# The four w_k transfers on ACT's queue, beside SP's w_mod transfers

## The chip, the cores and the metric

The kernel runs on one core of a Trainium2 chip. The metric is the device time of one launch in microseconds (us), as the median of several runs. A profile is one execution recorded by the hardware profiler; its times are counted from the start of its span.

## The reference

One block on x (2048 tokens, 512 features), all in float32: a linear attention (32 heads of 16) and a gated MLP that mixes over the tokens, each behind a layer norm whose scale, shift and gate come from a condition vector c.

```
mod = (silu(c) @ w_mod) -> sa, ca, ga, sb, cb, gb        # six vectors of 512
h = layernorm(x) * (1 + ca) + sa
q, k, v = h @ wqkv;  phi(t) = where(t > 0, t + 1, exp(t)) + 1e-6
o = phi(q) (phi(k)^T v) / (phi(q) sum phi(k) + 1e-6)     # per head
x = x + ga * (o @ wo)
h = layernorm(x) * (1 + cb) + sb
z1, z2 = halves of gelu(h @ w_in);  g = w_sp @ layernorm(z2) + b_sp
x = x + gb * ((z1 * g) @ w_out)
```

## The kernel before

Tokens are worked in 16 tiles of 128. Every float32 matmul operand is split into a high and a low part, and three matmuls (high by high, high by low, low by high; lines 110, 111 and 112) make one product. Before the first token tile can be multiplied, the kernel folds the condition into the projections: it needs `silu(c)` (`si`, lines 176 to 181), the vector ca as a column (`cm`, line 194, one call for each of the four 128-row parts of `w_mod[1]`), the same as a broadcast tile `cbr` on ACT (`mc`, line 326), the column means of the weights (`mr`, line 332, four calls for w_k, then four for w_q), and then on DVE the scaled weights (`wf`, line 336), which ACT and DVE split into the high and the low part (`qh`, line 340, and `qd` or `qg`, line 343). The first token matmuls are `kk1,0` and so on (lines 110 to 112, tile `kp`).

The order of all work is written out by hand in strings of short words (`ORDER`, `ORDER3`), and each engine runs its instructions in that order. `lm m,kc` loads part kc of `w_mod[m]`, `lk kc` loads part kc of w_k (the second of the three planes of `w_qkv`), `lw 0,h` a half of w_q, `ly t` a transposed tile of x (`xt`), `lx t` a plain one (`x`). `th t` and `tl t` split `xt` (ACT, line 399; DVE, line 402). `du` words are dummy matmuls on a tile of ones (line 172). All transfers are issued by SP: `dma = nc.sync.dma_start` at line 106, and the four of w_k through `load_part` at line 154, which `load_m` uses too. In the first line of `ORDER` the w_k loads stand behind the four loads of `w_mod[1]` and the words that use them:

```
si lm1,0 du1 du2 du3 du4 cm1,0 lm1,1 cm1,1 lm1,2 cm1,2 lm1,3 cm1,3 mc lk0 lk1 ly1 th1 tl1 lk2 lk3 du5
mr1,0 ly0 th0 tl0 lm0,0 mr1,1 mr1,2 lw0,0 lw0,1 ce1 mr1,3 wf1,3 qh1,3 qg1,3 mr0,0 ...
```

Buffers are chosen by hand as well: `SLOTS` holds for each pool one character for each tile that is asked for, in order, and that character names the buffer. A tile waits until the tile that held its buffer before has been read for the last time. The pool "zs" has 16 buffers and 83 requests.

Of the kernel before, what the change touches and what calls it, by code (L numbers as in the profile page):

```python
# [26 lines left out]
def block_kernel(ctx: ExitStack, tc: tile.TileContext, x, x_t, w_qkv, w_o, w_in, w_sp, b_sp, w_out,  # L27
                 w_out_tail, c, w_mod, ident_c, mask_c, out):
    nc = tc.nc

    def pool(name, bufs, space=None, stack=None):
# [27 lines left out]
            "25401567342067341564730642734206"  # L59
        ),  # L60
        "psb": "10101010010101001110101010101101010101",
        "zs": "0fe12dcba34987652dcb24a38b9a6cd8b4a3b838c4b6ca34cb34b4c3b4c30fe17b259d68a043cd6c0f1",
        "tb": (
            "065431260412304516230614250416450454653165013431423165104163421435241536211654063052141630516453"
            "0662635436360140660606656611141260606231515015"
# [18 lines left out]
    def sb(tag, shape, dt, name):  # L84
        return pools[tag].tile(shape, dt, tag=slot(tag), name=name)
# [20 lines left out]
    dma = nc.sync.dma_start  # L106
# [29 lines left out]
    RAW = {}  # L136
# [10 lines left out]
        XR[t] = sb("ta", [P, KC, P], F32, f"xt{t}")  # L147
        dma(XR[t], x_t[t])

    def load_part(key, src, kc, tag):  # L150
        k = key + (kc // 2,)
        if k not in RAW:
            RAW[k] = sb(tag, [P, 2, D], F32, "raw_" + "_".join(map(str, k)))
        dma(RAW[k][:, kc % 2], src[:, kc])

    def load_w(j, h):
        load_raw(("qkv", j, h), w_qkv[j, :, 2 * h:2 * h + 2, :])

    def load_wk(kc):
        load_part(("qkv", 1), w_qkv[1], kc, "st")  # L160

    def load_m(m, kc):
        load_part(("mod", m), w_mod[m], kc, "zs")
# [365 lines left out]
    def win_lo(h, kc, eng=nc.gpsimd):  # L529
# [4 lines left out]
    OPS = {  # L534
        "lx": load_x, "lw": load_w, "lm": load_m, "li": load_ident, "du": lambda k: dummy(2), "si": silu,
        "ly": load_xt, "lk": load_wk, "s1": s1, "bh": s2_hi, "bl": s2_lo, "cm": col_mm, "cr": col_part, "ce": col_end,
        "mc": mean_col, "mr": mean_mm, "wf": w_mid,
        "cv": lambda: (col_part("v"), col_end("v")), "mv": lambda m, k: mod_vec(m, k, k + 1), "vp": v_prod, "va": v_add,
# [232 lines left out]
    def hx_lo(t):  # L771
# [13 lines left out]
        "l5": lambda: load_mod(5, "s4"),  # L785
    })
    ORDER = """
        si lm1,0 du1 du2 du3 du4 cm1,0 lm1,1 cm1,1 lm1,2 cm1,2 lm1,3 cm1,3 mc lk0 lk1 ly1 th1 tl1 lk2 lk3 du5
        mr1,0 ly0 th0 tl0 lm0,0 mr1,1 mr1,2 lw0,0 lw0,1 ce1 mr1,3 wf1,3 qh1,3 qg1,3 mr0,0 yp0,0 lm0,2 wf1,1
        wf1,2 qh1,1 wf1,0 mr0,1 qh1,0 qd1,0 qg1,1 mr0,2 mr0,3 lm0,1 yp0,1 ya0,1 wf0,0 ly3 th3 qh1,2 qd1,2 lx0  # L790
        kk1,0 kk1,1 yp0,2 lm0,3 yp0,3 ya0,2 ya0,3 s10 ly2 kk0,0 kk0,1 wf0,1 wf0,2 th2 tl2 kk0,2 qh0,1 lx1
# [374 lines left out]
```

## Time and profile before

| | |
|---|---|
| median of 3 runs | 623.53 us (622.91 to 624.8) |
| profiled execution, its own time | 625.56 us |
| its span | 623.5 us |
| TensorE (PE) busy | 615.2 us, 99% of the span |
| VectorE (DVE) busy | 483.8 us, 78% |
| ScalarE (ACT) busy | 328.9 us, 53% |
| granted TensorE clock | 1.00 |
| read from HBM, written | 66.07 MB, 25.95 MB |

In the views, PE is the matmul stream and PEld its weight loads; SPq is the queue of SP, where a row is the time of issuing a transfer, not of the transfer. "to landing" counts from the issue to the arrival of the last byte. A bracket behind a row tells how long the engine sat idle before it and what ended that. The names of the rows are `raw_mod` for the parts of `w_mod`, `raw_qkv` for the parts of `w_qkv`, `pcol` for the column, `wm` for the means, `wf` for the scaled weights, `wk` and `wq` for their split parts.

### The profile page before, as it was taken

The page shows a single profiled execution, that of the slowest core. Times are in us where ns is not written, and L with a number is a line of the kernel's source. Part 1 is how long each engine was busy: PE and PEld are TensorE (multiplying, and loading weights), DVE is VectorE, ACT ScalarE, POOL GpSimd, SP SyncE. Part 2 cuts the span into 40 slices and gives each one's busy share as a digit, 9 for nine tenths or more (in the row PEclk, how much of TensorE's full clock was granted, in tenths as well). Part 3 has the DMA queues.
Part 4 walks back from the last instruction along what each step waited for, and adds up shares of the span by engine and source line. Part 5 has one row for each costly group of instructions (what it writes and reads, how often), then busy time and mean ns, then how long its engine had stood idle before and what let it go on. Part 6 is the DMA issues. An engine that isn't in the chain of part 4 may idle for free.

```text
span 623.5 us, 9515 instructions
## 1 busy us (share of the span) xinstructions
PE 615.2 (99%) x3383; PEld 559.2 (90%) x3383; DVE 483.8 (78%) x910; ACT 328.9 (53%) x556; POOL 221.8 (36%) x185
## 2 busy tenths in 40 slices
PE   8999999999999999999999999999999999999998
PEld 6678888787899999999999999999999999988886
DVE  2989997888888877877845689898799887886762
ACT  2768794656566476545647253654444354453320
POOL 0742354635866657553434504021223012400000
PEclk9999999999999999999999999999999999999999
DMA  8352422450337566746852966545575664889871
GB/s 275 147 185 79 156 91 74 125 158 33 102 92 177 138 168 178 202 145 191 234 181 80 307 235 209 152 139 107 171 204 169 188 159 145 239 282 272 265 260 67
DMA packets 91310, 105.74 MB, mean 170 GB/s; under 512 B 57120, under 2 KB 57632, under 8 KB 91264
## 3 DMA queue, kind: packets, MB, share of 16 engines
q1 hardware_dynamic: 91264, 105.15, 56.6%
q8 instruction: 26, 0.43, 0.3%
q14 instruction: 20, 0.16, 0.1%
HBM read 66.07 MB, written 25.95 MB: 148 GB/s over the span
## 4 chain that ended last, share of the span: by engine, by line
PE 80%; DMA 8%; DVE 7%; issue 2%; ACT 1%; SPq 0%; ACTq 0%; DVEq 0%
PE z L650 19%; PE P L928 17%; PE Pq L928 10%; PE pout L111 3%; PE pout L112 3%; PE pout L110 3%; PE po L110 2%; PE po L111 2%; PE po L112 2%; DMA raw_qkv<-in_w_qkv 2%; PE g L112 2%; PE qp L111 2%; PE qp L112 2%; PE g L110 2%; PE g L111 2%; PE qp L110 2%
## 5 line engine op out<-in xcount | busy, mean ns | idle before, releaser
L650 PE MATMUL z<-win,ht 128*128 128x344 f32 x768 | 122.7, 320 | 0.0
L650 PEld LDWEIGHTS z<-win,ht 128*128 128x128 f32 x768 | 121.5, 189 | 0.7
L928 PE MATMUL P<-z,f 128*128 128x344 f32 x576 | 96.3, 321 | 0.3
L928 PEld LDWEIGHTS P<-z,f 128*128 128x128 f32 x576 | 91.5, 188 | 1.5 <-DVE f L918 1.2
L918 POOL TENSOR_TENSOR f<-raw_wsp,f 128x512 fp32r<-128x512 f32 x24 | 35.9, 1509 | 148.4 <-ACT f L915 128.5
L928 PE MATMUL Pq<-z,wsp 128*128 128x344 f32 x384 | 61.3, 321 | 0.0
L928 PEld LDWEIGHTS Pq<-z,wsp 128*128 128x128 f32 x384 | 61.0, 188 | 0.0
L254 POOL TENSOR_TENSOR mv<-ve,mhalf 128x1 f32<-128x1 f32 x48 | 36.4, 760 | 41.8 <-DVE ve L253 30.5
L915 ACT ACTIVATE f<-raw_wsp 128x512 fp32r<-128x512 f32 x48 | 29.3, 626 | 32.3 <-DMA raw_wsp<-in_w_sp 12.9
L470 POOL TENSOR_TENSOR pksum<-pksum,tk 128x512 f32<-128x512 f32 x15 | 22.8, 1517 | 49.4 <-DVE tk L442 45.3
L915 ACT ACTIVATE f<-sa 128x512 fp32r<-128x512 f32 x36 | 22.5, 629 | 33.3 <-DVE sa L908 7.8
L268 ACT COPY uca<-us 128x768 uint16<-128x768 uint16 x32 | 25.1, 829 | 19.0 <-DVE us L983 12.2
L686 POOL TENSOR_TENSOR z<-zz,z 128x688 fp32r<-128x688 f32 x16 | 28.4, 1789 | 16.8 <-ACT z L683 16.8
L111 PE MATMUL pout<-wout,ut 128*128 128x512 f32 (+1 forms) x85 | 32.5, 382 | 0.6 <-DVE wout L1048 0.6
L110 PE MATMUL pout<-wout,ut 128*128 128x512 f32 (+1 forms) x85 | 32.4, 381 | 0.0
L112 PE MATMUL pout<-wout,ut 128*128 128x512 f32 (+1 forms) x85 | 32.3, 380 | 0.0
L1017 ACT ACTIVATE ut<-ur 128x384 fp32r<-128x384 f32 x32 | 15.2, 517 | 31.1 <-DMA ur<-ud 14.2
L918 DVE TENSOR_TENSOR f<-sa,f 128x512 fp32r<-128x512 f32 x36 | 26.0, 726 | 6.2 <-ACT f L915 6.0
L111 PE MATMUL qp<-wq,ht 128*128 128x512 f32 x64 | 25.3, 395 | 0.6 <-DVE wq L343 0.6
L110 PE MATMUL kp<-wk,ht 128*128 128x512 f32 x64 | 25.9, 404 | 0.0
L579 POOL TENSOR_TENSOR prod<-pq,zrep 128x512 f32<-128x512 f32 x16 | 21.4, 1342 | 11.7 <-ACT zrep L705 4.2
L112 PE MATMUL g<-pkhl,hhl 128*128 128x512 f32 x64 | 25.3, 395 | 0.2 <-DVE hhl L394 0.2
(254 smaller groups left out, 1500.1 us busy)
## 6 DMA issues: line engine op xcount, KB each, us to landing
raw_wsp<-in_w_sp SPq DMA_DIRECT2D x32, 512.0 KB, 4.5
ud<-uca SPq DMA_DIRECT2D x16, 384.0 KB, 3.1
ur<-ud SPq DMA_DIRECT2D x16, 384.0 KB, 4.5
z1d<-z SPq DMA_DIRECT2D x16, 344.0 KB, 2.5
zd<-zz SPq DMA_DIRECT2D x16, 344.0 KB, 3.0
z1r<-z1d SPq DMA_DIRECT2D x16, 344.0 KB, 3.7
xt<-in_x_t SPq DMA_DIRECT2D x16, 256.0 KB, 3.7
x<-in_x SPq DMA_DIRECT2D x16, 256.0 KB, 2.8
```

What stands on the lines that cost most here:

```text
L110: mm(o, a_hi, b_hi, start=first, stop=False, **kw)
L111: mm(o, a_hi, b_lo, start=False, stop=False, **kw)
L112: mm(o, a_lo, b_hi, start=False, stop=last, **kw)
L254: nc.gpsimd.tensor_tensor(mv[:, 1:2], ve, mhalf, op=OP.pow)
L268: nc.scalar.copy(pl[:, h], v[:, :, h])
L470: nc.gpsimd.tensor_add(pksum, pksum, PK[t])
L579: nc.gpsimd.tensor_mul(pr, PQ[t], KV["z"])
L650: mm(p[:, b, :HB], a[:, i, kc], win[h][:, j, kc, b * HB:(b + 1) * HB], start=kc == 0 and k == 0, stop=kc == KC - 1 and k == 2)
L686: nc.gpsimd.tensor_sub(Z2[t][:, 1], ZZ[t], f(Z2[t][:, 0]))
L915: nc.scalar.activation(SF[p, h, k][:, 0], s_src(p, h, k), AF.Copy)
L918: eng.tensor_sub(SF[p, h, k][:, 1], s_src(p, h, k), f(SF[p, h, k][:, 0]))
L928: mm(B[key][:, :HB], a[:, x_], b[:, y_], start=i == 1, stop=i == n)
```

## The change

The four `lk` words move to the very front of `ORDER`, ahead of `si`, and their transfers are issued from ACT's queue (`nc.scalar.dma_start`). Nothing else of the order changes. The string of the pool "zs" is written anew.

```
-        "zs": "0fe12dcba34987652dcb24a38b9a6cd8b4a3b838c4b6ca34cb34b4c3b4c30fe17b259d68a043cd6c0f1",
+        "zs": "0fed1234cba9876512341acb849c63284acb48b83a463cba34ba4a3b4a3b0fed74159268c0ab32630fd",
...
-    def load_part(key, src, kc, tag):
+    def load_part(key, src, kc, tag, q=dma):
...
-        dma(RAW[k][:, kc % 2], src[:, kc])
+        q(RAW[k][:, kc % 2], src[:, kc])
...
-        load_part(("qkv", 1), w_qkv[1], kc, "st")
+        load_part(("qkv", 1), w_qkv[1], kc, "st", nc.scalar.dma_start)
...
-        si lm1,0 du1 du2 du3 du4 cm1,0 lm1,1 cm1,1 lm1,2 cm1,2 lm1,3 cm1,3 mc lk0 lk1 ly1 th1 tl1 lk2 lk3 du5
+        lk0 lk1 lk2 lk3 si lm1,0 du1 du2 du3 du4 cm1,0 lm1,1 cm1,1 lm1,2 cm1,2 lm1,3 cm1,3 mc ly1 th1 tl1 du5
```

## The prediction, made before the changed kernel had run

> **What bounds the kernel now.** I read the page first, for the engine that is full, and then busy time by stretches, for where it is not.
>
> ```profile
> PE 615.2 (99%) x3383; PEld 559.2 (90%) x3383; DVE 483.8 (78%) x910; ACT 328.9 (53%) x556; POOL 221.8 (36%) x185
> ...
> 0.00:18.00 18.00, 14.96 (x69) 10.50 (x69) 5.40 (x10) 6.47 (x12) 2.98 (x9) 1.00 0.85 292
> 18.00:31.00 13.00, 12.39 (x57) 9.46 (x55) 12.26 (x26) 10.30 (x20) 9.04 (x8) 1.00 0.28 101
> 31.00:120.00 89.00, 89.00 (x384) 71.94 (x385) 77.62 (x150) 65.04 (x104) 40.63 (x35) 1.00 0.38 121
> ```
>
> The columns of the stretches are the length, then the busy time of PE, PEld, DVE, ACT and POOL, the granted clock, the DMA share and GB/s. From 31 us to 120 us PE has no idle time at all: what the start gains or loses up to 31 us goes through to the end. So the case is decided in the first 31 us, and I follow the chain of preparation there, engine by engine, in order of time. First SP's issues and the times to landing (in each answer the transfers of the one short stretch in which they are issued):
>
> ```profile
> 0.73 0.40 SPq L116 DMA_DIRECT2D cT<-in_c  x1
> 1.19 1.84 SPq L154 DMA_DIRECT2D raw_mod<-in_w_mod  x4
> 3.07 0.91 SPq L154 DMA_DIRECT2D raw_qkv<-in_w_qkv  x2
> 4.02 0.43 SPq L148 DMA_DIRECT2D xt<-in_x_t  x1
> 4.49 1.00 SPq L154 DMA_DIRECT2D raw_qkv<-in_w_qkv  x2
> ...
> raw_mod<-in_w_mod SPq DMA_DIRECT2D x1, 256.0 KB, 5.0
> ...
> raw_qkv<-in_w_qkv SPq DMA_DIRECT2D x1, 256.0 KB, 6.3
> ...
> raw_qkv<-in_w_qkv SPq DMA_DIRECT2D x1, 256.0 KB, 6.6
> ```
>
> The three landing rows are of the fourth w_mod part (issued at 2.6, three steps of 0.46 behind 1.19), of lk1 (issued at 3.5) and of lk2 (issued at 4.49). They land at 7.6, 9.8 and 11.1 us. The reader is to see that the issues run far ahead of the landings: SP is done issuing w_mod at 3.03 us and the data comes up to 5 us later. The transfers move one behind the other, and the stream of data is the limit, not the issuing:
>
> ```profile
> 2.00:4.00 2.00, 2.00 (x11) 2.00 (x11) 0.51 (x3) 0.21 (x2) 0.00 (x0) 1.00 0.64 181
> 4.00:6.00 2.00, 1.81 (x16) 1.65 (x16) 0.00 (x0) 0.00 (x0) 0.00 (x0) 1.00 0.96 304
> 6.00:8.00 2.00, 1.99 (x17) 1.80 (x16) 0.00 (x0) 0.00 (x0) 0.00 (x0) 1.00 0.94 275
> 8.00:10.00 2.00, 1.76 (x13) 1.39 (x12) 0.00 (x0) 0.60 (x1) 0.00 (x0) 1.00 0.99 338
> ...
> 12.00:14.00 2.00, 1.23 (x3) 0.19 (x1) 0.90 (x2) 0.69 (x2) 0.00 (x0) 1.00 0.93 364
> 14.00:16.00 2.00, 1.16 (x3) 0.68 (x4) 2.00 (x4) 1.51 (x3) 0.81 (x1) 1.00 1.03 407
> ```
>
> The DMA engines are 0.94 to 0.99 busy from 4 us on. Now what the landings release (PEld, PE, ACT, DVE in turn):
>
> ```profile
> 7.68 0.97 PEld L194 LDWEIGHTS pcol<-sil,raw_mod 128*128 128x128 f32 x8 [0.20 <-DMA raw_mod<-in_w_mod]
> ...
> 11.15 0.39 PEld L332 LDWEIGHTS wm<-raw_qkv,cbr 128*128 128x128 f32 x2 [0.47 <-DMA raw_qkv<-in_w_qkv]
> ...
> 4.68 4.16 PE L194 MATMUL pcol<-sil,raw_mod 128*128 128x128 f32 x32 [0.19 <-DMA raw_mod<-in_w_mod]
> ...
> 9.53 3.70 PE L332 MATMUL wm<-raw_qkv,cbr 128*128 128x512 f32 x8 [0.24 <-ACT cbr L326]
> 14.85 3.67 PE L332 MATMUL wm<-raw_qkv,cbr 128*128 128x512 f32 x8 [1.62 <-DMA raw_qkv<-in_w_qkv]
> ...
> 17.95 0.79 PE L110 MATMUL kp<-wk,ht 128*128 128x512 f32 x1
> ...
> 30.91 0.50 PE L111 MATMUL qp<-wq,ht 128*128 128x512 f32 x1 [0.60 <-DVE wq L343]
> ...
> 13.10 0.69 DVE L402 TENSOR_TENSOR ht<-xt,ht 128x512 fp32r<-128x512 f32 x1 [1.28 <-ACT ht L399]
> 13.71 2.72 DVE L336 SCALAR_TENSOR_TENSOR wf<-raw_qkv,col,wm 128x512 f32<-128x512 f32 x4
> 17.12 1.12 DVE L343 TENSOR_TENSOR wk<-wf,wk 128x512 fp32r<-128x512 f32 x1 [0.70 <-ACT wk L340]
> 18.61 0.75 DVE L336 SCALAR_TENSOR_TENSOR wf<-raw_qkv,col,wm 128x512 f32<-128x512 f32 x1 [0.36 <-PE wm L332]
> ```
>
> The last w_mod part lands at 7.6; its eight passes, the dummies and `cbr` follow, and the means of w_k start at 9.53, 1.93 us behind that landing. They take 3.70 us although w_k's third part lands only at 11.1; the means of w_q, at 14.85, take 3.67 us with all but one of their loads in place. So waiting for w_k costs nothing today: w_mod is what these means wait for. They end at 13.23; the scaled weights start at 13.71, held 0.48 us by the split of `xt` in front of them. From there DVE is busy up to 31 us (12.26 of the 13 us behind 18 us), and at 30.91 PE still waits for it. That is the path.
>
> **The change, part by part.** *The zs string.* Position by position it is one renaming of the buffers (1 to d, 2 to 1, d to 2, c to 3, b to 4, a to c, 3 to b, 4 to a, the rest unchanged), so every tile follows the same tile as before: no wait is added or lost. Cost nothing.
>
> *SP.* Four issues of about 0.46 us go (0.91 and 1.00 us for each two). The w_mod issues stand ahead of them and stay at 1.19 to 3.03. What comes later on SP moves up, but it enters a stream that is full, so by itself this brings nothing on the path; `xt`, w_q and x find it fuller or emptier by no more than the 0.46 us below.
>
> *ACT.* It now issues four transfers first. No row shows an issue on ACT; the nearest is SP's, 0.40 to 0.50 us each, so they run from 0.73 to about 2.6. Behind them come the table load and the exponential:
>
> ```profile
> 0.72 1.28 ACT L178 ACT_TABLE_LOAD   x1 [0.72 <-PEq L1158]
> ...
> 2.44 0.20 ACT L178 ACTIVATE e<-cT 128x4 f32<-128x4 f32 x1 [0.43 <-DMA cT<-in_c]
> ...
> 3.09 0.16 DVE L181 TENSOR_TENSOR sil<-cT,e 128x4 f32<-128x4 f32 x1
> ```
>
> The exponential then starts at 2.6 + 1.28 = 3.9 and `sil`, ready 0.81 us after its start (3.25 - 2.44), comes at 4.7 instead of 3.25. The first w_mod part was used at 4.68 and can only come later now, so this hides behind the data. Should ACT's issues take twice as long, `sil` comes at 6.5, still ahead of the last part.
>
> The profile cannot say whether the table load would stay in front of the issues. The Trainium skill, page "ScalarE: Activation LUTs", section "Step-by-step: what each stage is for", says that the compiler places the load right before the activation that needs it; the load's line here, L178, is the exponential's, which agrees. By that rule the issues come first; the other order is a rival below.
>
> *The data.* This is the term that counts. Eight parts of 256 KB (w_mod and w_k, 2.1 MB) are now all asked for between 0.73 and 3.0 us. Today the order of arrival is w_mod 1 to 4, lk0, lk1, `xt`, lk2: the eighth lands at 11.1. Whether the two queues are served in turns or in order of issue, the fourth w_mod part (2.6) is asked for after the fourth w_k part (2.1), so it becomes the eighth. The bounds of its landing are 7.6 (w_k takes nothing from it) and 11.1 (eighth, stream unchanged). I take the upper end less the earlier start of the stream, 1.19 - 0.73 = 0.46: 10.6 us, because the engines are already 0.94 to 0.99 busy and have no room for w_k beside w_mod.
>
> No row of before has two queues at work. The Trainium skill, page "DMA: Bandwidth & Descriptors", section "Issuing engines are not separate DMA queues", says that transfers issued by ACT and SP run on the same 16 DMA engines and interleave, and that a second issuer saves only the issuing time; its section "Queues, rings and completion order" adds that an engine takes turns between queues packet by packet. By these w_mod pays for w_k's bytes, the upper bound; the busy shares above are this case's sign for it.
>
> *The sum.* Landing at 10.6; means of w_k at 10.6 + 1.93 = 12.6; their end at 12.6 + 3.67 = 16.2; scaled weights at 16.2 instead of 13.71: 2.5 us later (`xt` lands in time: it is ninth and tenth, near 12 us, and its split no longer stands in the way). DVE's idle 0.36 us ahead of 18.61 goes, since the means of w_q now end before it: they follow the last pass of the w_k means at about 16.0 and end by 19.7, while DVE is busy with `wk` up to 20.7. The 0.70 us wait for ACT stays. Left at 30.91: 2.5 - 0.36 = 2.2 us, and PE, full from 31 us on, carries it to the end. The profiled execution would take 625.56 + 2.2 = 627.8; it stood 2.0 us over the median of the runs. The median: 623.53 + 2.2 = 625.7 us, 0.35% more.
>
> About 0.3%, 1.9 us, is what a measurement of this kernel can tell from no change.
>
> **The rivals.**
>
> *Two queues move data faster (no change).* From 4 to 8 us the engines were busy at 275 to 304 GB/s, from 14 us at 407. If the slow start is one queue's own, 2.1 MB take 5.2 us at 407; from about 1.9 us, plus the 1.4 us from the last byte moved (9.7, adding up the stretches) to the landing at 11.1, the last part lands at 8.5: the scaled weights start at 14.1, 0.4 us late, which DVE's 0.36 us swallow: 623.6. For it: nothing but the rate; against it: the later 407 are of one queue too. 10%.
>
> *w_mod stays ahead (not slower, or less).* With the table load first, ACT issues from 2.0 us, and the fourth w_mod part is the sixth in line: lk1's landing today, 9.8. That is 9.8 + 1.93 + 3.67 = 15.4, 1.7 late, 1.3 at the end: 624.9. If w_k took nothing from w_mod at all, the means would run from 9.53 as now, and the most to be won is the 0.48 us ahead of 13.71: 623.05. The point from which this side decides: a landing before 8.1 us. 10%.
>
> *PE loses its clock (slower still).* The w_mod passes ran without a break from 4.68 to 8.84; they would come in four bursts of about 1 us with as much idle between. At half the clock the means of w_k alone would cost another 3.7 us: 629.4. Against it: the granted clock was 1.00 from 12 to 16 us with PE busy 1.23 and 1.16 of 2 us. The Trainium skill, page "TensorE: Matmul & The Clock Gate", Part 1, says that the clock is halved after an idle window of some 3.4 us; no run here shows one, and by that rule the gaps of about 1 us would not do it. Milder, on the same side: two queues that hinder each other, or issues on ACT that take longer, and bring the last part another 1 us later (626.7). Together 15%.
>
> **How the numbers follow.** The forecast has 60%, with 1.7 to 2.7 us by its landing between 10.1 and 11.1; five in six of that lies over 1.9 us. Slower: 50 + 15 = 65%. Within 0.3%: 10 + 10 + 10 = 30%. Faster by over 0.3%: 5%, for a shift of the order later that no row shows; the start can win 0.5 us at most. The range runs from the first rival, 623.6, to the hindered queues with a spread, 627.4; the lost clock and the real gain stay out.
>
> **What would show it.** Right: four ACT issues ahead of the table load; the last w_mod part landing near 10.6 and the w_k parts before it; means of w_k at 12.6, scaled weights at 16.2, first `kp` at 20.4, and PE's wait for `wq` at 33; the same DMA rate; clock 1.00. Wrong: the last w_mod part landing before 9 us, a rate near 400 GB/s from 4 to 8 us, or a shift at 31 us that is gone at 120 us.

## The result, and the profile after

The changed kernel takes 629.47 us (median, 627.99 to 630.71) against 624.09 us before; the ratio is 1.0073, 95% interval [1.0055, 1.0091], some 4.5 us more. The direction was as forecast, the size was twice the 2.2 us forecast, and 629.47 lies over the range. The profiled execution of after took 628.36 us, with a span of 626.5.

The first fence is the timeline of the changed kernel's first 24 us, the issuing queues and the engines in order; then the times to landing of cT, of the first and of the fourth w_mod part, each from the answer for the stretch in which it is issued; last, the issue of the fourth w_mod part alone and what SP waited for ahead of it.

```profile
0.72 2.09 ACTq L154 DMA_DIRECT2D raw_qkv<-in_w_qkv  x4
0.73 0.40 SPq L116 DMA_DIRECT2D cT<-in_c  x1
0.98 3.78 PE L172 MATMUL warm<-ones 128*128 128x128 f32 x16 [0.98 <-POOL ones L120]
1.18 4.98 SPq L154 DMA_DIRECT2D raw_mod<-in_w_mod  x4
2.84 1.28 ACT L178 ACT_TABLE_LOAD   x1 [2.84 <-issue]
6.01 0.20 ACT L178 ACTIVATE e<-cT 128x4 f32<-128x4 f32 x1 [1.89 <-DMA cT<-in_c]
...
7.30 6.76 PE L194 MATMUL pcol<-sil,raw_mod 128*128 128x128 f32 x32 [2.54 <-DMA raw_mod<-in_w_mod]
...
14.75 7.13 PE L332 MATMUL wm<-raw_qkv,cbr 128*128 128x512 f32 x16 [0.24 <-ACT cbr L326]
...
18.55 2.72 DVE L336 SCALAR_TENSOR_TENSOR wf<-raw_qkv,col,wm 128x512 f32<-128x512 f32 x4 [2.00 <-issue]
...
cT<-in_c SPq DMA_DIRECT2D x1, 2.0 KB, 5.3
...
raw_mod<-in_w_mod SPq DMA_DIRECT2D x1, 256.0 KB, 6.0
...
raw_mod<-in_w_mod SPq DMA_DIRECT2D x1, 256.0 KB, 4.5
...
5.83 0.33 SPq L154 DMA_DIRECT2D raw_mod<-in_w_mod  x1
...
SPq L154 <- DMA raw_qkv<-in_w_qkv: 3.0, 1, 3.0
```

The four w_k issues take 2.09 us on ACT, and the table load stands behind them, both as forecast. The fourth w_mod part is issued at 5.8, not at 2.6 as forecast: SP waits 3.0 us for the landing of the first w_k part, whose semaphore (the counter that reports a landing) this ninth transfer takes over; the eight before it have one each. It lands at 10.4 (5.83 and 4.5); 10.6 was forecast. But cT, a transfer of 2 KB, lands at 6.0 instead of 2.4. The first w_mod part lands at 7.2 instead of 4.5. And when PE starts on w_mod at 7.30, the 32 passes take 6.76 us instead of 4.16. The means of w_k start at 14.75; 12.6 was forecast, and 9.53 it was before.

Why the passes are longer is seen in the durations of one pass. The fence has two answers on line L194, of before and then of after (columns: instances, minimum, median and maximum in ns, first and last start), and then the dummies that run between 4.0 and 4.3 us, again before and then after.

```profile
L194 PE MATMUL pcol<-sil,raw_mod x32: 273/273/377, 4.7 to 8.6; 128*128 128x128 f32 x32
L194 PE MATMUL pcol<-sil,raw_mod x32: 272/421/553, 7.3 to 13.8; 128*128 128x128 f32 x32
...
L172 PE MATMUL warm<-ones x4: 274/316/421, 3.7 to 4.2; 128*128 128x128 f32 x4
...
L172 PE MATMUL warm<-ones x3: 421/421/421, 3.7 to 4.1; 128*128 128x128 f32 x3
```

The same pass takes 273 ns when PE is warm and 421 ns when it is cold. Passes overlap, so the time from one to the next differs more: 32 in a row take 6.76 us here, 0.21 us each, and 3.81 us, 0.12 each, in a warm run below. Before, PE went warm at 3.9 us, among the dummies, and w_mod followed at once. After, the dummies ended at 4.76 before PE was warm, PE then stood idle for 2.54 us, and all but the last few of the w_mod passes ran cold (up to 13.4 us). The column of the granted clock does not show this (busy time by stretches, after; the seventh value is the clock):

```profile
4.00:6.00 2.00, 0.76 (x4) 0.47 (x3) 0.00 (x0) 0.12 (x1) 0.00 (x0) 1.00 0.90 262
6.00:8.00 2.00, 0.70 (x3) 0.73 (x4) 0.51 (x3) 0.20 (x1) 0.00 (x0) 1.00 1.06 406
8.00:10.00 2.00, 2.00 (x12) 2.00 (x10) 0.00 (x0) 0.00 (x0) 0.00 (x0) 1.00 1.03 390
```

It reads 1.00 while the passes take 421 ns and more. What follows carries the delay to the end: PE's wait for `wq`, and the matmuls of line L650, first in before and then in after (the after row of the wait answers to the one at 30.91).

```profile
35.67 0.50 PE L111 MATMUL qp<-wq,ht 128*128 128x512 f32 x1 [0.61 <-DVE wq L343]
...
L650 PE MATMUL z<-win,ht x768: 314/320/402, 179.5 to 334.5; 128*128 128x344 f32 x192
L650 PE MATMUL z<-win,ht x768: 314/320/404, 184.2 to 339.3; 128*128 128x344 f32 x192
```

The shift is 4.84 us at the scaled weights, 4.76 at 35.67, 4.7 at 179.5. The two profiled spans differ by only 3.0, because that execution of before lost time late: from 520 to 570 us every other profile of this document gains 0.6 to 1.8 us on it. The ratio, some 4.5 us, agrees with 4.7.

### The profile page after: what moved, and what is told of

The parts are those of the page before. It is cut to its first block, busy times and chain, and to the rows that moved or that the text cites. A ratio compares the mean times of both kernels' runs of the same rounds, so it can differ in the third digit from the quotient of the medians.

```text
span 626.5 us, 9514 instructions
## 1 busy us (share of the span) xinstructions
PE 617.1 (98%) x3383; PEld 562.0 (90%) x3383; DVE 485.6 (78%) x910; ACT 328.3 (52%) x556; POOL 220.3 (35%) x185
## 4 chain that ended last, share of the span: by engine, by line
PE 83%; DVE 9%; DMA 3%; issue 2%; ACT 2%; SPq 0%; ACTq 0%; DVEq 0%
PE z L650 19%; PE P L928 19%; PE Pq L928 10%; PE pout L111 3%; PE pout L112 3%; PE pout L110 3%; PE po L112 2%; PE po L111 2%; PE po L110 2%; DMA raw_mod<-in_w_mod 2%; PE g L112 2%; PE qp L111 2%; PE qp L112 2%; PE g L110 2%; PE g L111 2%
## 5 line engine op out<-in xcount | busy, mean ns | idle before, releaser
L650 PE MATMUL z<-win,ht 128*128 128x344 f32 x768 | 122.7, 320 | 0.0
L650 PEld LDWEIGHTS z<-win,ht 128*128 128x128 f32 x768 | 121.5, 189 | 0.8
L111 PE MATMUL kp<-wk,ht 128*128 128x512 f32 x64 | 25.4, 396 | 0.7 <-DVE wk L343 0.7
L1070 DVE TENSOR_TENSOR x<-x,pout 128x512 f32<-128x512 f32 (+1 forms) x17 | 10.8, 655 | 19.2 <-PE pout L1066 11.7
L110 PE MATMUL kp<-wk,ht 128*128 128x512 f32 x64 | 25.5, 399 | 0.1
```

The source lines that it names most:

```text
L110: mm(o, a_hi, b_hi, start=first, stop=False, **kw)
L111: mm(o, a_hi, b_lo, start=False, stop=False, **kw)
L650: mm(p[:, b, :HB], a[:, i, kc], win[h][:, j, kc, b * HB:(b + 1) * HB], start=kc == 0 and k == 0, stop=kc == KC - 1 and k == 2)
```

## The experiments

The theory after the result: w_mod lands behind w_k's bytes because w_k is asked for first, whoever issues it, and PE is cold when w_mod comes, so that its passes take longer as well. The rivals: the second queue costs by itself; the late cT is the cause; a cold PE is no term of its own; the renamed buffers cost something. The table has the landing of the last w_mod part (issue and time to landing, to 0.1), the start and length of the w_mod passes, the starts of the means of w_k and of the scaled weights (us, from each profile), and the ratio to before.

| kernel | last w_mod part | w_mod passes | means | scaled weights | ratio, 95% interval |
|---|---|---|---|---|---|
| before | 7.6 | 4.68, 4.16 | 9.53 | 13.71 | 1 |
| after | 10.4 | 7.30, 6.76 | 14.75 | 18.55 | 1.0073 [1.0055, 1.0091] |
| order of after, all on SP | 11.0 | 8.67, 5.58 | 14.94 | 18.75 | 1.0074 [1.0062, 1.0086] |
| the same, PE kept warm | 11.2 | 9.36, 3.81 | 13.85 | 17.65 | 1.0045 [1.0027, 1.0063] |
| after, PE kept warm | 11.1 | 7.14, 5.33 | 13.15 | 16.96 | 1.0048 [1.0032, 1.0064] |
| after, silu without c | 11.2 | 7.43, 6.54 | 14.66 | 18.45 | 1.0070 [1.0053, 1.0087] |
| after, cT first on ACT | 9.6 | 8.46, 6.36 | 15.50 | 19.30 | 1.0067 [1.0046, 1.0088] |
| after, w_k behind silu | 9.4 | 4.93, 5.64 | 11.25 | 15.63 | 1.0022 [1.0006, 1.0037] |
| before, no dummies | 7.5 | 4.57, 5.42 | 10.67 | 14.47 | 1.0004 [0.9991, 1.0016] |
| before, new zs string | 7.3 | 4.57, 4.59 | 9.85 | 13.65 | 0.9988 [0.9978, 0.9998] |
| before, w_k ahead of xt | 7.7 | 4.56, 4.87 | 10.12 | 13.93 | 1.0004 [0.9993, 1.0015] |

**Order without the second queue.**

```
 (after)
-        load_part(("qkv", 1), w_qkv[1], kc, "st", nc.scalar.dma_start)
+        load_part(("qkv", 1), w_qkv[1], kc, "st")
```

> The order of the changed kernel (w_k asked for ahead of w_mod), but all transfers on SP's queue as before, cT first. It parts the order from the second queue. Theory (w_mod landing behind w_k's bytes is the cost, whoever issues, and PE is cold by then): cT lands at 2.4, the first w_mod part is fifth in line and lands near 8.3, PE has idled from 4.7 and runs the passes at 421 ns at first; the means of w_k start between 13.0 (warm) and 15.7 (cold throughout); median 627.5 to 630. Rival (the cost is the second queue, by the late cT and the slow start of two queues): median below 626.

The issues, the exponential and the passes in that kernel's timeline:

```profile
0.73 0.40 SPq L116 DMA_DIRECT2D cT<-in_c  x1
1.18 1.84 SPq L154 DMA_DIRECT2D raw_qkv<-in_w_qkv  x4
3.07 1.85 SPq L154 DMA_DIRECT2D raw_mod<-in_w_mod  x4
...
2.39 0.20 ACT L178 ACTIVATE e<-cT 128x4 f32<-128x4 f32 x1 [0.38 <-DMA cT<-in_c]
...
8.67 5.58 PE L194 MATMUL pcol<-sil,raw_mod 128*128 128x128 f32 x32 [3.90 <-DMA raw_mod<-in_w_mod]
```

Ratio 1.0074, the same as the whole change. With one queue cT is early and the issues are undisturbed, yet w_mod comes later still and PE is cold again, for the first half of the passes (it is warm from 12.2 us on). So the order alone is enough for a loss of this size; against this order the second queue made no difference that can be told. That the two come out so equal is partly chance: the passes start 1.4 us later than in after and take 1.2 us less.

**The same order with PE kept warm, and the change with PE kept warm.**

```
 (order on SP)
-        "lx": load_x, ... "du": lambda k: dummy(2), ...
+        "lx": load_x, ... "du": lambda k: dummy(6 if k < 5 else 2), ...
 (after)
+        "lx": load_x, ... "du": lambda k: dummy(4 if k < 5 else 2), ...
```

> The order of the changed kernel with all transfers on SP, and 48 dummy passes instead of 16 ahead of the w_mod passes, so that PE is kept busy up to about 8.6 us, when the first w_mod part lands. It is the case that the prediction reckoned with: w_mod behind w_k, PE warm. Theory (what is left is the data term): the last w_mod part lands near 10.9, the means of w_k start 1.93 us behind it, at 12.8 instead of 14.94, the scaled weights at 16.5; about 2.1 us less than the same order with 16 dummies (629.1), so 627.0, 2.8 us over before. Rival (the cold PE is no term of its own): 629.

> The changed kernel with 32 dummy passes instead of 16 ahead of the w_mod passes. Theory (a cold PE sets the length of the w_mod passes, 421 ns each instead of 273): the dummies fill PE up to about 6.6 us, the passes run at 273 ns and wait for the last w_mod part at 10.2, the means of w_k start near 12.1 instead of 14.75; median about 2.6 us less than the changed kernel's 629.5, so 626.9. Rival (the data or silu(c) sets it): no change, 629.5.

The passes of L194 with the order on SP, and then the first passes with after's transfers (line and timeline views of the two kernels; the last row is a weight load, which shows a wait that the merged row of the 24 passes hides):

```profile
L194 PE MATMUL pcol<-sil,raw_mod x32: 273/273/348, 9.4 to 12.9; 128*128 128x128 f32 x32
```

```profile
0.98 5.75 PE L172 MATMUL warm<-ones 128*128 128x128 f32 x32 [0.98 <-POOL ones L120]
7.14 1.13 PE L194 MATMUL pcol<-sil,raw_mod 128*128 128x128 f32 x8 [0.41 <-DMA raw_mod<-in_w_mod]
9.12 3.35 PE L194 MATMUL pcol<-sil,raw_mod 128*128 128x128 f32 x24 [0.85 <-DMA raw_mod<-in_w_mod]
...
10.41 1.86 PEld L194 LDWEIGHTS pcol<-sil,raw_mod 128*128 128x128 f32 x16 [0.33 <-DMA raw_mod<-in_w_mod]
```

In both the passes are warm, and more work on PE makes the kernel shorter: from 1.0074 to 1.0045, and from 1.0073 to 1.0048, the scaled weights 1.1 and 1.6 us earlier. The intervals within each pair touch or overlap; it is that both pairs and both timelines say the same that makes the cold PE a term of its own. The rest, 2.8 and 3.0 us, is the data; the 2.2 of the forecast lies inside both intervals (1.7 to 3.9 and 2.0 to 4.0 us). Both means started later than expected (13.85 for 12.8, 13.15 for 12.1), for a reason told below.

**Whether the late cT is the cause.** Two kernels, and the first missed its aim.

```
 (after)
-    dma(cT, c)
+    nc.scalar.dma_start(cT, c)
 (after)
-        nc.scalar.activation(e0, cT, AF.Exp, scale=-1.0)
+        nc.scalar.activation(e0, f(ones[:, :KC]), AF.Exp, scale=-1.0)
 ...
-        nc.vector.tensor_mul(sil, cT, e0)
+        nc.vector.tensor_copy(sil, e0)
```

> The changed kernel with the transfer of cT issued first on ACT's queue, ahead of w_k, instead of first on SP's. Theory (the first w_mod part lands at 7.2 us and PE has gone cold by then; the late silu(c) is covered by that): cT lands near 2.5, sil is ready near 5.3 instead of 6.8, but the passes still start at about 7.2 at 421 ns each; median unchanged within 0.5 us, 629.5. Rival (the late landing of cT is the cause): the passes start near 5.4 and the median falls by about 1.9 us, to 627.6.

```profile
0.72 0.40 ACTq L116 DMA_DIRECT2D cT<-in_c  x1
1.15 5.11 ACTq L154 DMA_DIRECT2D raw_qkv<-in_w_qkv  x4
6.29 1.28 ACT L178 ACT_TABLE_LOAD   x1 [6.29 <-DMA cT<-in_c]
...
cT<-in_c ACTq DMA_DIRECT2D x1, 2.0 KB, 5.2
```

cT, though first in its queue, again took 5.2 us to land, and the fourth w_k issue, ahead of the table load, waited for it, so silu came later (the passes start at 8.46), not earlier. The expected landing at 2.5 was wrong, and the ratio, 1.0067, decides nothing on the question. It shows another thing: here nothing held the fourth w_mod part; it was issued at 2.13 and landed at 9.6, ahead of the last two w_k parts.

> The changed kernel, but silu is taken of the tile of ones instead of cT, so that nothing waits for cT (the condition is left out of the result; the same instructions run, but for one DVE copy in place of a multiply). The run before this one that was to do that held ACT back instead. Theory (the first w_mod part, landing at 7.2, starts the passes, and PE is cold by then): silu is ready near 5, the passes start at 7.2 at 421 ns; median unchanged within 0.5 us of the changed kernel, 629.5. Rival (the late cT is the cause): the passes start near 5 and the median falls by 2 us.

```profile
5.10 0.17 DVE L181 COPY sil<-e 128x4 f32<-128x4 f32 x1
...
7.43 6.54 PE L194 MATMUL pcol<-sil,raw_mod 128*128 128x128 f32 x32 [2.67 <-DMA raw_mod<-in_w_mod]
```

Here silu is ready at 5.27, and the passes still start with the first w_mod part, at 7.43, and still cold. The ratio is 1.0070: the late cT is not the cause, it lies beside the late w_mod.

**w_k on ACT, but behind silu.**

```
 (after)
-        lk0 lk1 lk2 lk3 si lm1,0 ...
+        si lk0 lk1 lk2 lk3 lm1,0 ...
```

> The four w_k transfers stay on ACT's queue, but their words stand behind si, so ACT issues them after the exponential that waits for cT. Theory (w_mod and cT pay for w_k being asked for ahead of them, and PE goes cold while it waits): cT lands at 2.4 us again and the first w_mod part near 4.7, the w_mod passes stay at 273 ns, the means of w_k start at 9.5 to 10.5 instead of 14.75; median 624 to 625.5. Rival (a second queue costs by itself, wherever it stands): median stays near 629.

```profile
2.50 7.21 ACTq L154 DMA_DIRECT2D raw_qkv<-in_w_qkv  x4
4.93 3.11 PE L194 MATMUL pcol<-sil,raw_mod 128*128 128x128 f32 x24 [0.27 <-DMA raw_mod<-in_w_mod]
9.41 1.16 PE L194 MATMUL pcol<-sil,raw_mod 128*128 128x128 f32 x8 [1.36 <-DMA raw_mod<-in_w_mod]
...
14.40 4.56 PE L332 MATMUL wm<-raw_qkv,cbr 128*128 128x512 f32 x10 [0.30 <-DMA raw_qkv<-in_w_qkv]
```

With w_mod asked for first, the first three parts come about as before and PE is warm. The fourth still lands 1.7 us later than in before, at 9.4, behind w_k's first part (9.15). ACT's last issue is held to past 9 us, until that fourth w_mod part has landed, and the means wait for the w_k part that it loads (14.40). Ratio 1.0022, median 626.16 and so a little over the 625.5 expected: most of the loss is gone with the queue unchanged, so the rival of a queue that costs it all by itself falls here too. What remains is w_k's first part in w_mod's way, and that held issue.

**A cold PE in the kernel before.**

```
 (before)
-        si lm1,0 du1 du2 du3 du4 cm1,0 ...
+        si lm1,0 cm1,0 ...
```

> The kernel before without the 16 dummy passes ahead of the w_mod passes (du1 to du4 left out; they write a tile that nobody reads). Nothing else moves, so this prices a cold PE by itself. Theory: the 32 w_mod passes take 421 ns each and about 6.8 us instead of 4.16, the means of w_k start near 12.1 instead of 9.53; median 2.2 us over before, 626.3. Rival (the length of the passes is set by the data): same as before, 624.1.

```profile
4.57 5.42 PE L194 MATMUL pcol<-sil,raw_mod 128*128 128x128 f32 x32 [4.57 <-DMA raw_mod<-in_w_mod]
```

The passes take 1.26 us more, not 2.6: PE went warm after 3.3 us of work, in the middle of them. The scaled weights are 0.76 us late, and the ratio cannot tell that from no change. A miss in size; the sign is seen in the timeline alone.

**The zs string alone.** (before, with the line of after)

> The kernel before with the new string of the pool zs and nothing else. Theory (the string only renames buffers, each tile follows the same tile): same time as before, 624.8, and the same first 31 us. Rival (the new places cost something, in addresses or waits): over 626.

Ratio 0.9988 [0.9978, 0.9998], with nearly the same first 31 us but for a PE that went warm later (the passes take 4.59 us, the means start 0.3 us later, the scaled weights do not). Slower it is not; the 0.1% to the other side is at the edge of what can be told, and no row explains it.

**A version meant to beat both.**

```
 (before)
-        ... mc lk0 lk1 ly1 th1 tl1 lk2 lk3 du5
-        mr1,0 ly0 th0 tl0 lm0,0 ... wf1,0 mr0,1 qh1,0 qd1,0 ...
+        ... mc lk0 lk1 lk2 lk3 ly1 th1 tl1 du5
+        mr1,0 ly0 th0 lm0,0 ... wf1,0 mr0,1 qh1,0 tl0 qd1,0 ...
```

> A version meant to beat both: the kernel before with lk2 and lk3 issued on SP directly behind lk1, ahead of the transposed x tile, and the split tl0 moved behind the scaled weights, into DVE's idle 0.70 us. w_mod stays first. The scaled weights start at 13.2 instead of 13.71, so 0.5 us less: 624.3 against 624.8, within what can be told from no change. Rival (DVE and ACT are met later by the moved split): no gain, or up to 0.7 us more.

No gain: in the profiled execution the second w_mod part landed late (PE waited 0.76 us), and the scaled weights started at 13.93. Of the rival something is seen too: the moved split ran from 16.57 to 17.26 on DVE, and the first split of w_k behind it ended at 18.93, 0.7 us later than in before. How much each of the two took away was not parted. The kernel before stays the best.

## Why the prediction was wrong in size

**What held.** The start decides, and PE, full behind 31 us, carries the shift on; w_mod is what the means wait for, and w_k was not; ACT's issues come ahead of the table load and take 2.09 us; the last w_mod part lands eighth (10.4, forecast 10.6); the renaming costs nothing. On the rule that two issuers interleave on the same DMA engines (the Trainium skill, page "DMA: Bandwidth & Descriptors", section "Issuing engines are not separate DMA queues"), the runs agree: the order with one queue and with two comes out alike, 1.0074 and 1.0073, and in after the parts of the two queues land in turn, w_k at 7.0, w_mod at 7.2, w_k at 8.1, w_mod at 8.7.

**Luck in the landing.** 10.4 is near 10.6, but not by the way that was reckoned. The w_mod issues were to stay at 1.19 to 3.03; the fourth was held to 5.8. Where it was not held (cT first on ACT), it landed seventh, at 9.6. And with the same transfers as after it landed at 11.1 and 11.2 in two other kernels (PE kept warm; silu without c).

**The step that failed: from the last landing to the means, taken as 1.93 us.** That price was read where PE was warm and was done with three parts when the fourth landed. It was carried over although w_mod would come later, and a cold PE was put at nothing in the sum. After, the step takes 4.4 us (10.4 to 14.75): PE starts at 7.30, works through the parts cold and is done only at 14.06, when the last has long landed; the weight loads of the 32 passes follow one another without a wait. The sum should have run from the first landing through 32 cold passes. Unrounded, it forecast the scaled weights at 16.24; they start at 18.55, 2.3 us later. Of that the earlier landing is -0.3, this step +2.5, and the stretch from the means to the scaled weights +0.1 (3.80 instead of 3.67).

With PE kept warm on the transfers of after, the step is 2.0 us (11.1 to 13.15), as the prediction had it: PE waits for the second and the third part (0.85 and 0.33 us in the rows above), so the data sets the end again. That kernel's scaled weights, at 16.96, are 0.7 us over the forecast mostly because its last part landed 0.5 us later than 10.6. So the step fails by the cold PE. What the cold PE costs is 1.6 us by the two starts of the scaled weights (18.55 and 16.96), and some 2.3 us by an estimate that takes the step of 2.0 from the landing of 10.4 (12.4 instead of 14.75).

In the order on SP with PE kept warm the step is 2.7 us: there the four parts land 0.65 us apart (9.2 to 11.2), closer than eight warm passes take (0.9 us), and all 32 run in one row. Parts that land close together are thus a smaller term of the same step, 0.7 us in that kernel.

**The rival that was turned down: "PE loses its clock".** It was refused on the granted clock of 1.00 and on gaps too short. The first reason was wrong: the column shows 1.00 for cold passes too, in before as well (its dummies at 421 ns); a pass's duration was the thing to read. The second missed the point. Short gaps did leave a warm PE warm (1.36 us ahead of 9.41 with w_k behind silu, 1.25 us ahead of 9.36 with the order on SP), but in after PE did not lose its pace: with 16 dummies ending at 4.76 it had not yet reached it. It went warm at 3.9 us, 2.9 us after the first dummy, in one execution of the kernel before, and only near 6.0 with the new zs string, where nothing else differs; without a gap before w_mod that hardly matters. That the rival's price gave 629.4, and 629.47 was measured, is luck: it charged 3.7 us to the means of w_k, which ran warm (16 passes in 7.13 us, as 8 in 3.70 before), and the loss was in the w_mod passes. The Trainium skill, page "TensorE: Matmul & The Clock Gate", Part 1, says that activity is judged in windows of 3.4 us that do not start with the kernel, and that this moves the change by half a microsecond either way. The delays seen here spread wider: 2.9 us and 5.0 us from the first dummy (before, and with the new zs string), 6.1 us from the first w_mod pass in after.

**The term that came back: DVE's 0.36 us.** The wait ahead of the first scaled weights of w_q did go (23.02 follows at once). But the split behind it, 0.70 us before, takes 1.12. The rows are of DVE's and of POOL's timelines, in each before and then after:

```profile
19.28 0.70 DVE L343 TENSOR_TENSOR wk<-wf,wk 128x512 fp32r<-128x512 f32 x1
...
23.68 1.12 DVE L343 TENSOR_TENSOR wk<-wf,wk 128x512 fp32r<-128x512 f32 x1
```

```profile
18.12 1.30 POOL L226 TENSOR_TENSOR yp<-yp,yp 128x512 f32<-128x512 f32 x1 [0.42 <-ACT yp L222]
19.90 2.68 POOL L226 TENSOR_TENSOR yp<-yp,yp 128x512 f32<-128x512 f32 x2 [0.47 <-ACT yp L222]
...
22.62 4.71 POOL L226 TENSOR_TENSOR yp<-yp,yp 128x512 f32<-128x512 f32 x3
```

Before, this split ran from 19.28 to 19.98 and POOL was idle from 19.42 to 19.90; after, POOL sums beside it without a break. The other kernels agree: the split takes 0.83 us where POOL pauses for 0.4 us beside it (w_k ahead of xt), 0.94 where it pauses for 0.2 us (new zs string), and 1.12 where it does not pause (before without dummies). That the overlap is the cause is read from these rows and was not tried alone.

So 2.2 + 2.3 + 0.36 = 4.9 us, against 4.76 at 35.67 and about 4.5 from the ratio. *Covered, as argued:* silu came 2.1 us later than reckoned (6.8, not 4.7), by a cT whose landing was taken as unchanged without a row for it, but the first w_mod part was later still. The chance of "five in six" is four in five if the range of 1.7 to 2.7 us is spread evenly; nothing hangs on it.

## What to carry to other kernels

Here the transfers filled the DMA engines, and a second queue did not bring the data in sooner by more than one execution differs from the next. In such a stretch the first thing to be used should be the first to be asked for: moving a load ahead of it delayed it by those bytes, from one queue as from two. Where loads move, ask what the waiting engine does meanwhile. A PE that has not yet worked long enough took 0.21 us for a pass instead of 0.12, and then its own passes, not the last landing, set the end. Read that pace from the duration of one pass, not from the clock column.

## What was not expected of the hardware

A 2 KB transfer of 16-byte rows landed in 1.7 us with the first bulk transfer issued 0.46 us behind it, and in 4.3 to 5.3 us in the four kernels where a bulk transfer of another queue was issued within 0.01 us of it, on either queue. Which part of the path holds it was not tried. The data also started more slowly with two queues: 139 GB/s from 2 to 4 us against 181 before, then 406 from 6 to 8 us against 275. A busy share of 0.94, at 275, was thus not yet the most that the engines move. The first eight parts were in at 10.4 us against 11.1, but at 11.1 and 11.2 in the two other kernels with the same transfers as after.
